# Attention and ELU feed-forward on one core: second scores joined to the next pair's tails, values into the product banks

## The chip, the cores and the metric

One core of a Trainium2 chip (trn2). The time is that of one execution on the device, in microseconds, as the median of several; lower is better. The engines are TensorE (PE; PEld is its weight load), VectorE (DVE), ScalarE (ACT), GpSimd (POOL) and SyncE (SP, which here only issues DMAs). TensorE writes to PSUM, eight banks of 512 fp32 columns on 128 partitions.

## What is computed

Threshold attention over 8 sequences of 8 heads, 576 rows of 64, and behind it a feed-forward network with an ELU, 512 to 2048 to 512, over the 4608 rows:

```python
def _attn_ref(q, k, v, tau):
    scale = 1.0 / np.sqrt(q.shape[-1])
    scores = scale * np.matmul(q, k.transpose(0, 1, 3, 2))
    thresh = np.max(scores, axis=-1, keepdims=True) - tau
    scores = np.where(scores >= thresh, scores, -1000000000.0)
    scores = scores - np.max(scores, axis=-1, keepdims=True)
    attn = np.exp(scores)
    attn = attn / (np.sum(attn, axis=-1, keepdims=True) + 1e-09)
    return np.matmul(attn, v).astype(np.float32)

def _moe_ref(x, w_in, w_out):
    h = x @ w_in
    g = np.where(h > 0.0, h, alpha * (np.exp(np.minimum(h, 0.0)) - 1.0))
    return (g @ w_out).astype(np.float32)
```

All data are fp32. Between the two, heads become columns: row (b, s) of x holds the 8 heads of that row.

## The kernel before

**Pairs.** Two heads of one sequence are a pair; there are 32, `pr` 0 to 31, four to a sequence. A pair's 576 query rows are four blocks of 128 (`i` = 0 to 3) and a tail of 64 for each head, which together make block `NC` = 4. Head h lies on partitions 64h to 64h + 63 of `qT` and `kT`.

**One block of scores** goes like this: TensorE writes 128 x 576 scores per head into PSUM (`wide_scores` L785, for the two blocks of a half, `half` 0 being blocks 0 and 1; `tails_and_values` L829 for the tails, L852). VectorE takes the negated row maximum (`wide_max` L807, at L809), POOL the threshold (`wide_bounds`, L818), ScalarE the exponential (`wide_exp`, L822) into one of two buffers (`turned_by`: `w_one` and `e`), VectorE masks and sums (`wide_mask`, L826), sums and inverts (L554, L560); POOL normalizes (L503); VectorE turns it by 32 x 32 (`turn_squares` L644, at L649 and L662), SP writes it to DRAM in pieces (`there`) and a later `fetch` (L689) reads it back transposed. Two pairs after its scores, `tails_and_values` multiplies it with v: the 64 tail rows first (L857, weights `vd`), then the four blocks (`values_main`, L865), part 1 ahead of part 0. `values_out` (L870) has ScalarE copy the result into `xt`, the input of the feed-forward network, and for part 1 into `xs`, which a DMA takes to `xtail`.

**TensorE's shapes.** Matmuls run on parts of the array. Scores, tails and the value products of the tail rows (L857) are 64x64 (four at once); the blocks' values and the FFN products of the loop (`by_columns`, L772) are 128x64 (two column halves at once). In the early stage FFN products are 128x128 (L924, L952, L992).

**PSUM.** One tile of five banks, `wide` (`sc` in the profile), takes scores, tails and values: a half's scores columns 64 to 2368; the tails banks 3 and 4, the values banks 1 and 2 before the first half's scores overwrite them. Three more banks, f0, f1 and f2 (`f`), go in turn to the FFN products (`ends`, a rotating list). `on_banks` (L744) keeps, for each bank, what touched it last on each engine, and makes an instruction wait for the other engines' accesses of its own banks alone; the tracking of the whole tile is turned off for them.

**Two stages.** The first 250 us or so (`early_tasks`, L1096: sequence 0, pairs 4 to 8, conversion of the weights, the first feed-forward rows) run jobs in an order written out by hand (`EARLY`). Jobs name what they need; `banked` hands a job's last instruction on each engine to those that need it. There a half is two jobs, `wsc.pr.half.0` and `.1`, and all jobs of the next step wait for `users`, the masks and value copies of the step before. Between the two parts of a half stands `seen` (L805), a copy of one column by ScalarE.

From pair `START` = 9 on a loop (L1798) issues work by a planned clock: `on_pe` puts a TensorE step at the planned time and moves the clock by its planned length, and everything else is put down with a due time (`at`), to be issued in the order of these times; `MOVED` and `FIRST` shift single due times. The engines wait for each other by semaphores alone, so the plan only sets the order in each engine's queue. One turn of the loop: the tails of pair pr with the values of pair pr - 2 (`tail_step` L1725); the first half of pair pr (`wide_step` L1741); 14 FFN quarters (`ffn_quarters` L1692); the second half; 14 quarters. A quarter is four matmuls of 256 columns: a seventh of a first product (`first_product` L1466, x times w_in by a scheme of seven products) or half of one of the second round's fourteen (`second_round` L1596). `sums_x` (L1086) makes the five sums of x that a group of first products needs, once a sequence.

Inputs of the next pair are turned (`prep_q`, `prep_k`) and loaded at times set from the two halves. Behind the loop the last sequence and the tails' rows have a stage of their own, in which the five banks of `wide` join the rotation.

Of the kernel before, what the change touches and what calls it, by code (L numbers as in the profile page):

```python
# [20 lines left out]
    "9:3.0": 0.61, "9:fetch0": -3.6, "9:turn4": 2.44, "e:139.1": 0.46, "e:140.2": -0.49, "e:176.2": 1.07,  # L21
    "e:203p0": 1.03, "e:30.2": 0.35, "e:73p0": 1.88, "e:75p0": 1.3, "e:77.2": -1.81, "e:78.1": -3.94, "e:9b":
# [154 lines left out]
def kernel(  # L177
# [552 lines left out]
    def followed(ins, engine, needed):  # L730
# [10 lines left out]
        serials[ins.name] = engine, len(serials), dict(have)  # L741
        return kept_

    def on_banks(made, ap):  # L744

        ins, needed, starts = made.ins, [], [ap.offset % (5 * 512)]
        for step, n in ap.ap[1:-1]:
# [20 lines left out]
    def by_columns(o, left, right, note=None, **how):  # L768
        n = o.shape[0]
        for y in range(0, n, D):  # L770
            oy = o[y : y + D] if n > D else o
            made = nc.tensor.matmul(oy, left[:, y : y + D] if n > D else left, right, skip_group_check=True, **how)  # L772
            if note:
                note(made, oy)
# [1393 lines left out]
```

## Time and profile before

| what | us |
|---|---|
| median of 3 runs | 1258.58 (1257.97 to 1258.75) |
| the profiled execution, its own time | 1258.3 |
| its span (first to last instruction) | 1256.5 |
| PE busy | 1240.8 |
| DVE busy | 1067.2 |
| POOL busy | 790.5 |
| ACT busy | 584.4 |
| granted TensorE clock, mean | 1.00 |

Busy times are unions of an engine's instructions. TensorE's ends are modelled and overlap with the next start, so its pace is read from start to start. In the view of instructions in order of time, a row is a run of like instructions: start, length, engine, line, operation, out<-in, active rows*columns of the array, operand, count, and in brackets the idle time before with what ended it. An fp32 matmul of a part of the array leaves two records.

### The profile page before, as it was taken

Reading aid. Unit: us, or ns where it says so; the run is one execution under the profiler, and the core shown is the slowest. Engines: PE = TensorE matmul, PEld = TensorE weight load, DVE = VectorE, ACT = ScalarE, POOL = GpSimd, SP = SyncE. Lnnn points to the kernel's source line nnn. Section 1 sums busy time; section 2 is a strip of 40 time slices with the busy share of each in tenths; the row PEclk is TensorE's granted clock in tenths of the full one; section 3 lists DMA queues with packets and bytes.
Section 4 is the critical chain, followed back from the end, with each engine's and each line's share of the span. In section 5 each row is a group of like instructions: output and inputs, shape, how many; then the busy total and the mean of one; then the engine's idle time right before and its main releaser. Section 6 shows DMA issues by size and latency. Waiting matters only on the chain.

```text
span 1256.5 us, 32264 instructions
## 1 busy us (share of the span) xinstructions
PE 1240.8 (99%) x11999; PEld 825.9 (66%) x11999; DVE 1067.2 (85%) x2322; ACT 584.4 (47%) x1276; POOL 790.5 (63%) x1147
## 2 busy tenths in 40 slices
PE   8999999999999999999999999999999999999998
PEld 5776575466666666666666666666666666678887
DVE  7998989898889979898889888988989885777876
ACT  7987755453444435252625353444535260434130
POOL 5775545586576747674766657674767473675564
PEclk9999999999999999999999999999999999999999
DMA  8568899898979898998989898989899876444433
GB/s 224 152 182 248 217 253 256 239 303 217 257 208 268 231 242 229 262 245 240 238 226 266 230 257 202 265 232 240 227 257 248 238 214 224 163 140 152 137 113 115
DMA packets 332940, 278.31 MB, mean 221 GB/s; under 512 B 201328, under 2 KB 288368, under 8 KB 332784
## 3 DMA queue, kind: packets, MB, share of 16 engines
q1 hardware_dynamic: 331264, 275.57, 78.6%
q8 instruction: 94, 1.54, 0.5%
q10 hardware_dynamic: 1520, 0.69, 0.2%
q14 instruction: 62, 0.51, 0.1%
HBM read 178.85 MB, written 97.32 MB: 220 GB/s over the span
## 4 chain that ended last, share of the span: by engine, by line
PE 81%; DVE 2%; DMA 1%; POOL 1%; ACT 0%; issue 0%; SPq 0%; DVEq 0%; ACTq 0%; POOLq 0%
PE f L772 59%; PE sc L865 9%; PE sc L802 8%; PE f L992 2%; PE sc L857 1%; DMA there<-x 1%; PE sc L852 1%; PE f L924 1%; DVE mx L809 1%; DVE e L826 0%; DVE x L649 0%; DVE g L1536 0%; DVE g L1508 0%; SPq L668 0%; SPq L683 0%
## 5 line engine op out<-in xcount | busy, mean ns | idle before, releaser
L809 DVE TENSOR_REDUCE mx<-sc 128x1 f32<-128x576 f32 x252 | 180.0, 745 | 35.0 <-PE sc L802 30.3
L818 POOL TENSOR_SCALAR th<-mx,ntau 128x2 f32<-128x2 f32 (+1 forms) x140 | 45.9, 328 | 185.4 <-DVE mx L809 184.3
L822 ACT ACTIVATE w_one<-sc,mx 128x576 f32<-128x576 f32 x140 | 100.8, 740 | 131.9 <-DVE mx L809 110.3
L826 DVE SCALAR_TENSOR_TENSOR w_one<-sc,th,w_one 128x576 f32<-128x576 f32 x140 | 109.9, 812 | 20.2 <-ACT w_one L822 19.0
L802 PE MATMUL sc<-kT,qT 64*64 64x320 f32 (+5 forms) x1792 | 124.5, 410 | 2.1 <-DVE su L554 0.5
L772 PE MATMUL f<-xt,sw 128*64 128x256 f32 x1024 | 123.3, 382 | 0.7 <-ACT xt L432 0.5
L822 ACT ACTIVATE e<-sc,mx 128x576 f32<-128x576 f32 x112 | 82.8, 742 | 88.1 <-DVE mx L809 86.5
L772 PE MATMUL f<-x,w_in_sb 128*64 128x256 f32 x1024 | 123.1, 380 | 0.3 <-ACT g L1547 0.3
L772 PE MATMUL f<-xt,w_in_sb 128*64 128x256 f32 x1024 | 121.8, 379 | 0.5 <-DVE xt L1092 0.5
L503 POOL TENSOR_SCALAR w_one<-w_one,rs 128x576 f32<-128x576 f32 x115 | 89.3, 787 | 38.7 <-DVE rs L560 38.7
L649 DVE STREAM_TRANSPOSE x<-w_one 128x512 f32<-128x512 f32 (+1 forms) x140 | 99.9, 743 | 15.6 <-POOL w_one L503 9.6
L802 PEld LDWEIGHTS sc<-kT,qT 64*64 64x64 f32 x1792 | 80.9, 132 | 48.9 <-issue 18.5
L772 PE MATMUL f<-w_out_sb,s 128*64 128x256 f32 (+1 forms) x896 | 105.6, 377 | 0.0
L772 PE MATMUL f<-w_out_sb,g 128*64 128x256 f32 (+1 forms) x864 | 101.7, 376 | 0.0
L772 PEld LDWEIGHTS f<-x,w_in_sb 128*64 128x64 f32 x1024 | 74.4, 137 | 37.9 <-ACT g L1547 4.8
L772 PEld LDWEIGHTS f<-xt,w_in_sb 128*64 128x64 f32 x1024 | 75.4, 137 | 35.9 <-ACT e L822 0.9
L772 PEld LDWEIGHTS f<-xt,sw 128*64 128x64 f32 x1024 | 71.9, 137 | 41.1 <-issue 5.5
L826 DVE SCALAR_TENSOR_TENSOR e<-sc,th,e 128x576 f32<-128x576 f32 x112 | 87.6, 807 | 8.0 <-ACT e L822 7.7
L772 PE MATMUL f<-t,s 128*64 128x256 f32 (+1 forms) x800 | 93.5, 375 | 0.0
L772 PEld LDWEIGHTS f<-w_out_sb,s 128*64 128x64 f32 x896 | 63.7, 137 | 31.5 <-issue 3.2
L772 PEld LDWEIGHTS f<-w_out_sb,g 128*64 128x64 f32 x864 | 61.2, 137 | 31.7 <-issue 3.7
L503 POOL TENSOR_SCALAR e<-e,rs 128x576 f32<-128x576 f32 x92 | 67.8, 741 | 20.3 <-DVE rs L560 17.8
(324 smaller groups left out, 2807.9 us busy)
## 6 DMA issues: line engine op xcount, KB each, us to landing
there<-x SPq DMA_DIRECT2D x452, 144.0 KB, 3.7
wTb<-there SPq DMA_DIRECT2D x58, 576.0 KB, 6.2
wTa<-there SPq DMA_DIRECT2D x55, 576.0 KB, 4.9
sw<-win_sums SPq DMA_DIRECT2D x62, 384.0 KB, 4.0
t<-wout_sums SPq DMA_DIRECT2D x45, 512.0 KB, 5.2
there<-x SPq DMA_DIRECT2D x112, 80.0 KB, 2.0
wTb<-there SPq DMA_DIRECT2D x56, 160.0 KB, 3.8
wst<-in_moe_w_in_dram SPq DMA_DIRECT2D x16, 512.0 KB, 5.2
```

Of the source, the lines that this page charges most:

```text
L503: nc.gpsimd.tensor_scalar(wv, wv, st["rs"][:, h : h + 1], 1.0, ALU.mult, ALU.mult)
L649: nc.vector.transpose(x[:, :, c0 : c0 + nc_], src.rearrange("p (c g n) -> p g c n", c=nc_, n=T))
L772: made = nc.tensor.matmul(oy, left[:, y : y + D] if n > D else left, right, skip_group_check=True, **how)
L802: on_banks(nc.tensor.matmul(oy, qT[r, i * P + y * D : i * P + (y + 1) * D], kT[r, k0 : k0 + n], start=True, stop=True, skip_group_check=Tr ...
L809: on_banks(nc.vector.tensor_reduce(st["mx"][:, h : h + 1], st["sc", h], axis=AX.XY if i == NC else AX.X, op=ALU.max, negate=True), st["sc" ...
L818: nc.gpsimd.tensor_scalar(st["th"][:, cs], st["mx"][:, cs], -1.0, ntau, ALU.mult, ALU.add)
L822: on_banks(nc.scalar.activation(st["e", h], st["sc", h], AF.Exp, bias=st["mx"][:, h : h + 1]), st["sc", h])
L826: on_banks(nc.vector.scalar_tensor_tensor(st["e", h], st["sc", h], st["th"][:, h : h + 1], st["e", h], ALU.is_ge, ALU.mult, accum_out=st[" ...
L852: on_banks(nc.tensor.matmul(o, qT[r, MAIN:], kT[r, TAIL + x * HALF : TAIL + (x + 1) * HALF], start=True, stop=True, skip_group_check=True), o)
L857: on_banks(nc.tensor.matmul(o, vd[r, r], parts[x][r, g0:g1, NC], start=True, stop=False, skip_group_check=True), o)
L865: on_banks(nc.tensor.matmul(o, vm[:, h, c], parts[part][:, g0:g1, h * (NC + 1) + c], start=False, stop=(c == NC - 1), skip_group_check=Tru ...
L992: nc.tensor.matmul(cur[c, i][:, :DM], hidden(c, ft % NU, 1)[:, 0, ft // NU, i], w_out_sb[:, ft], start=(ft == 0), stop=(ft == NFT - 1))
```

## The change

- `wide` gets a sixth bank, which is f0; f1 and f2 stay tiles of their own.
- In the loop a turn becomes: the second half of pair pr - 1; the tails of pair pr with the values of pair pr - 2; 14 quarters; the first half of pair pr; 14 quarters. The second half is taken in another order (`seen_too`: block 3 first, buffers exchanged) and has a second `seen` copy.
- From START on tails and values go to places of their own (`tails_apart`): tail scores to columns 2368 to 2944 (the end of bank 4 and bank 5), cut at the bank's end into 192 and 384 columns; values to f1 and f2. The list of banks is set so that f2 comes first behind the values.
- In the early stage values go to banks 4 and 0 and tails to banks 2 and 3; the first part of a first half doesn't wait for the second value copy; `seen` is no longer handed on as a thing to wait for.
- `other_banks` and `beside` turn off tracking between products in the wide tile and scores or values in its other banks; accesses of the tails in bank 5 keep it.
- The sums of x are made in two halves, the first a pair earlier (for the first group by POOL in the early stage, jobs `xe`).
- Due times of maxima, exponentials, masks, sums, turns and fetches are planned anew, and `MOVED` and `FIRST` are other tables. Before the weight sums at the end the loop issues work until the last turns are out.

```diff
-    granted, banks_at_start = [None], {x: psum["f"].tile([P, 512], FP32, name=x) for x in ("f0", "f1", "f2")}
+    granted, banks_at_start = [None], {x: psum["f"].tile([P, 512], FP32, name=x) for x in ("f1", "f2")}
...
-    wide = [psum["w"].tile([P, 5 * 512], FP32, name="sc")]
-    banks_at_start["t"] = wide[0][:, 4 * 512 :]
+    wide = [psum["w"].tile([P, 6 * 512], FP32, name="sc")]
+    banks_at_start["f0"] = wide[0][:, 5 * 512 :]
+    banks_at_start["t"] = wide[0][:, 4 * 512 : 5 * 512]
...
-        if doing[0]:
+        if doing[0] and kept:
             banked.setdefault(doing[0], {})[engine] = ins
...
+        if (max(starts) + ap.ap[-1][1] - 1) // 512 < 5:
+            if apart:
+                other_banks(ins, "scores", "products")
+            else:
+                other_banks(ins, "values", "products", (nc.scalar, nc.vector))
+                other_banks(ins, "values", "outs")
...
-            st = open_step(pr, i, turned_by[1 - s])
+            st = open_step(pr, i, turned_by[s if seen_too else 1 - s])
...
         order = (((0, 0, 0, 448), (1, 1, 0, 320), (1, 1, 320, 256), (0, 0, 448, 128)),
+                 ((1, 0, 256, 320), (0, 1, 0, 384), (1, 0, 0, 256), (0, 1, 384, 192)) if seen_too else
                  ((1, 0, 0, 256), (0, 1, 0, 384), (1, 0, 256, 320), (0, 1, 384, 192)))
...
-            if (h, s, c) == (1, 1, 0):
-                on_banks(nc.scalar.copy(seen, o[:, :1]), o[:, :1])
+            if (h, s, c) == (1, 1, 0) or seen_too and (h, s, c) == (1, 0, 256):
+                on_banks(nc.scalar.copy(seen, o[:, :1]), o[:, :1], kept=False)
...
-        pv, sc = (wide[0].rearrange("p (x n) -> p x n", n=512)[:, b : b + 2] for b in (1, 3))
+        by_bank = wide[0].rearrange("p (x n) -> p x n", n=512)
+        pv, sc = [by_bank[:, 4], by_bank[:, 0]], by_bank[:, 2:4]
+        if pr is None or pr >= START:
+            return tails_apart(pr, before)
...
+    def tails_apart(pr, before):
+
+        places = [banks_at_start[x] for x in (("f2", "f1") if pr == START else ("f1", "f2"))] if before != NP - 1 else (wide[0][:, :512], wide[0][:, 512:1024])
+        sc = wide[0][:, 2 * T + 4 * S : 2 * T + 5 * S]
...
+        cut = 5 * 512 - 2 * T - 4 * S
+        for x, c, n in ((1, cut, S - cut), (0, 0, cut)):
+            for h in range(2):
+                r = slice(h * D, (h + 1) * D)
+                if before is not None:
+                    g0, g1 = span(h, x)
+                    o = places[x][r, g0 * T : g1 * T]
+                    watch(nc.tensor.matmul(o, vd[r, r], parts[x][r, g0:g1, NC], start=True, stop=False, skip_group_check=True), o)
+                if pr is not None:
+                    o = sc[D - h * D : P - h * D, c : c + n]
+                    on_banks(nc.tensor.matmul(o, qT[r, MAIN:], kT[r, TAIL + c : TAIL + c + n], start=True, stop=True,
+                                              skip_group_check=True), o)
...
+        for x, m in enumerate(X_ORDER):
+            job(("xe", m), "pool|dve", lambda e, m=m: sum_x(m, engine_of[e]), ("outv", START - 3, 0), ("outv", START - 3, 1), "late",
+                ("xe", X_ORDER[x - 1]) if x else None)
...
-                        ("wsc", pr, half, 0) if y else ("tail", pr) if not half else ("wsc", pr, 0, 1), *ready_of[pr], *users,
+                        ("wsc", pr, half, 0) if y else ("tail", pr) if not half else ("wsc", pr, 0, 1), *ready_of[pr],
+                        *[x for x in users if y or x[0] != "outv" or x[2]],
...
+            for x in ("f1", "f0", "f2") if pr == START else ("f2", "f0", "f1"):
+                ends.remove(banks_at_start[x])
+                ends.append(banks_at_start[x])
+
+        PLANS = ({(0, 0): (0.0, 1.6, 3.0), (0, 1): (0.75, 3.0, 4.3), (1, 1): (1.5, 4.7, 6.5), (1, 0): (2.25, 5.6, 6.9)},
+                 {(0, 0): (3.4, 7.7, 8.6), (0, 1): (5.1, 6.0, 7.5), (1, 1): (-0.8, 0.2, 1.2), (1, 0): (0.1, 1.0, 2.7)})
...
-                for x, i in enumerate((NC, 0, 1, 2, 3)):
-                    at(t + 6.0 + 3.8 * x, lambda pr=pr, i=i: fetch(pr - 1, i), f"fetch{i}")
+                for i, when in ((NC, 9.0), (0, 12.5), (1, 16.0), (2, 20.0), (3, 24.0)):
+                    at(t + when, lambda pr=pr, i=i: fetch(pr - 1, i), f"fetch{i}")
...
+            if START < pr <= NP:
+                wide_step(pr - 1, 1)
             tail_step(pr)
...
-            for half in range(2):
-                if pr < NP:
-                    wide_step(pr, half)
...
+            next_q(pr)
+            ffn_quarters(HALF_QUARTERS)
+            if pr < NP:
+                e = clock[0] + 2.15
+                wide_step(pr, 0)
+                next_k(pr)
+                extras(e + 0.3, e + 1.2, e + 4.2, e + 10.4, e + 12.0)
                 ffn_quarters(HALF_QUARTERS)
```

More of the change, by code (lines that the diff above doesn't have):

```diff
@@ L771, in by_columns, with watch, other_banks, beside @@
             oy = o[y : y + D] if n > D else o
-            made = nc.tensor.matmul(oy, left[:, y : y + D] if n > D else left, right, skip_group_check=True, **how)
-            if note:
-                note(made, oy)
-    def watch(made, ap):
+            (note or beside)(nc.tensor.matmul(oy, left[:, y : y + D] if n > D else left, right, skip_group_check=True, **how), oy)
+    def watch(made, ap, apart=True):
         if ap.tensor.name == wide[0].tensor.name:
-            on_banks(made, ap)
+            on_banks(made, ap, apart)
+    def other_banks(ins, mine, theirs, engines=(nc.tensor, nc.scalar, nc.vector)):
+        for e in engines:
+            if e.engine != ins.engine:
+                tc.declare_no_dep(ins, group=f"{theirs}{e.engine}", reason="other banks")
+        tc.add_to_no_dep_group(f"{mine}{ins.engine}", ins)
+    def beside(made, ap):
+        if ap.tensor.name == wide[0].tensor.name:
+            other_banks(made.ins, "products", "scores")
+            if made.ins.engine != nc.tensor.engine:
+                other_banks(made.ins, "products", "values", (nc.scalar, nc.vector))
+        return made
     def open_step(pr, i, w):
@@ L783, in open_step, with wide_scores @@
         return st
-    def wide_scores(pr, half, parts=(0, 1)):
+    def wide_scores(pr, half, parts=(0, 1), seen_too=False):
         qT, kT, _ = pairs[pr]
@@ L1499, in copy @@
                 loc[name] = kept(name)
-                nc.scalar.copy(loc[name], place(x))
+                beside(nc.scalar.copy(loc[name], place(x)), place(x))
             def pool(name, x, other, op):
@@ L1507, in add @@
             def add(o, x, name):
[L1508 removed]
+                beside(nc.vector.tensor_tensor(o, place(x), loc[name], ALU.add), place(x))
             def exp(c):
```

198 lines of the change are left out of this document (126 added, 72 removed), and 68 rows, old and new, of tables (FIRST, MOVED).

## The prediction

> **What bounds the kernel now.** I read the page first, then the time by stretch, then TensorE's rows in order of time, then its waits.
>
> The page's head, and the stretch view (columns: length, then busy time and instructions of PE, its weight loads, DVE, ACT, POOL; clock; DMA share; GB/s):
>
> ```profile
> span 1256.5 us, 32264 instructions
> PE 1240.8 (99%) x11999; PEld 825.9 (66%) x11999; DVE 1067.2 (85%) x2322; ACT 584.4 (47%) x1276; POOL 790.5 (63%) x1147
> ```
>
> ```profile
> 100.00:255.00 155.00, 151.77 (x950) 89.45 (x952) 138.31 (x288) 94.54 (x190) 84.72 (x116) 1.00 0.88 243
> 255.00:284.00 29.00, 28.00 (x274) 17.50 (x266) 26.84 (x59) 17.00 (x38) 23.14 (x33) 1.00 0.97 295
> 284.00:1040.00 756.00, 755.89 (x7476) 480.60 (x7476) 658.16 (x1448) 330.94 (x724) 491.00 (x741) 1.00 0.88 240
> ```
>
> TensorE has 0.1 us free in the 756 us of the pair loop, at full granted clock, and VectorE 98 us. So nothing there is gained by removing a wait: only work or pace of TensorE counts. Before 284 us there are a few waits. One pair in order of time (start, length, idle before):
>
> ```profile
> 403.33 1.90 PE L772 MATMUL f<-x,w_in_sb 128*64 128x256 f32 x16
> 405.16 2.17 PE L802 MATMUL sc<-kT,qT 64*64 64x448 f32 x32
> 407.26 1.95 PE L772 MATMUL f<-xt,sw 128*64 128x256 f32 x16
> 409.04 1.03 PE L772 MATMUL f<-x,sw 128*64 128x256 f32 x8
> 409.90 1.90 PE L772 MATMUL f<-xt,w_in_sb 128*64 128x256 f32 x16
> 411.63 2.00 PE L772 MATMUL f<-x,w_in_sb 128*64 128x256 f32 x16
> 417.77 1.90 PE L772 MATMUL f<-x,w_in_sb 128*64 128x256 f32 x16
> 419.60 0.45 PE L852 MATMUL sc<-kT,qT 64*64 64x288 f32 x1
> 420.73 2.37 PE L865 MATMUL sc<-wTb,vm 128*64 128x320 f32 x16
> 422.94 1.90 PE L865 MATMUL sc<-wTa,vm 128*64 128x256 f32 x16
> 424.76 2.17 PE L802 MATMUL sc<-kT,qT 64*64 64x448 f32 x32
> ```
>
> The reader is to look at starts, since modelled ends overlap. A group of 16 FFN records lasts 1.73 us (409.90 to 411.63). If 64x64 work follows, it lasts 1.83 (403.33 to 405.16, 417.77 to 419.60); the first one behind it lasts 1.78 (407.26 to 409.04). Changing between 128x64 and 64x64 shapes thus costs time that no wait shows.
>
> The early waits, then an early score step beside the loop's 2.17, and one wait of pair 9's first products:
>
> ```profile
> PE sc L852 <- ACT xs L432: 1.0, 1, 1.0
> PE sc L802 <- ACT xt L432: 0.5, 1, 0.5
> ```
>
> ```profile
> who waited for it (us, times):
>   PEld sc L802: 3.3, 10
> ```
>
> ```profile
> 200.97 2.46 PE L802 MATMUL sc<-kT,qT 64*64 64x448 f32 x32 [0.47 <-ACT xt L432]
> 210.54 2.46 PE L802 MATMUL sc<-kT,qT 64*64 64x448 f32 x32
> ```
>
> ```profile
> 259.83 1.08 PE L772 MATMUL f<-xt,w_in_sb 128*64 128x256 f32 x8 [0.52 <-DVE xt L1092]
> ```
>
> The middle fence is the view of the one-column copy "seen" (L805): ten times, all early, the array's weight load waited for it.
>
> **The change, part by part.** *Price of a 64x64 stretch.* 16 FFN records are 2 column halves at once, so 8 x 256 = 2048 column steps in 1.73 us, 0.845 ns a step. A half's scores are 1152 columns per quadrant in two passes, 2304 steps or 1.95 us; start to start it takes 2.10, so 0.15 too much, and with 0.10 ahead and 0.05 behind 0.30. The tails (576 columns, two passes, 0.97 us) take 1.13, again 0.16 too much. Check: a pair has 28 x 1024 + 4608 + 1152 + 2 x 2304 = 39,040 steps, 33.0 us, and takes 33.9 (tails start at 419.60, 453.44, 487.38, 521.22): 0.9 over for three stretches, again 0.30 each. Bounds 0.28 to 0.31.
>
> *Second scores put behind the products, in front of the next tails.* Before, a pair has three 64x64 stretches: tails, first half, second half. After, the second half's scores and the next pair's tails (with the 64-row value products beside them) form one, and the values run on into FFN products of their own shape. Matmuls and columns are equal in number. That happens for the second halves of pairs 9 to 31, 23 times: 23 x 0.30 = **6.9 us less** (6.4 to 7.1).
>
> *Where the tails and values go.* Tail scores move to the end of bank 4 and into bank 5, which is now f0; the values go to f1 and f2. Hence the next products wait for the evacuation. Count from the end of the second half's scores, h: tails until h+1.0, values 4.03 (2.21 and 1.82 by the rows above) until h+5.0, then a quarter each 0.86. f2 is needed at h+5.0: its values end at h+3.2, the copies take 0.37 and 0.42 (ACT), so 1.0 spare. f0 is needed at h+5.9 in a first product, h+6.7 in a second round. Its user is the tail's mask. In the changed program's order the longest DVE list from the second half's first maximum to that mask is three maxima (0.74 each), a turn in two instructions (1.44), two ELUs (about 0.67), the turn of q (0.77) and the mask (0.82), 6.6 us, and a second round follows. The plan begins it 0.8 before h; in the trace of before a half's first maximum begins 1.9 to 2.25 us after the scores begin, about at their end. So the mask ends between h+5.8 and h+6.7: 0.9 to 0 spare. In the other order of pairs it is three maxima and the mask, h+3.1 at most, 2.8 spare. Half the pairs may so wait some 0.1 us: I take **1.0 us more** over the loop, bounds 0 and 5 (0.2 a pair); the old loop met like deadlines (tail mask before the first half's scores, 4 us behind the tails) with 0.1 us of idle.
>
> *What else moves.* The turns of blocks 2 and 3, their DRAM writes and their fetches come later by what the second half is later against the pair's values: fetches are planned at 9, 12.5, 16, 20, 24 instead of 6 to 21.2 us, and the values start 3.3 us into the next pair rather than 1.1, so the last transfer keeps about its 12 us; it takes some 4 to 6 us (the page's landing times). On SP's queue they stand behind the writes of the same blocks. The qm, km and v loads keep their distance to their users. 23 more seen copies of 0.16 us stand on ACT (47% busy) ahead of the copies that empty products; a value copy or exponential behind them is 1 us later, within the spare above. Sums of x split in halves: 65 DVE instructions of 0.42 for 35 of 0.68, 3.5 us on an engine with 98 us free. Nothing for these; if their cover fails it shows as waits on f0 to f2, in the bounds above.
>
> *Early stage, same order on TensorE.* The seen copy is no longer a dependence: ten steps of 2.46 come to 2.17, 2.9 us (the copy's view says 3.3 with hidden parts). The first half no longer waits for the second value copy at pairs 6 and 7, 0.47 each plus 0.06: 1.1. Tail scores leave bank 4, so the wait of 1.0 at 116.9 us goes, but DVE is busy until 117.9 and the next scores wait for its mask: 0.2. Pair 9's two runs of 14 products take 13.07 and 13.16 against 12.24: 1.75, of which the sums of x, now half done on POOL earlier, are about half. Together 5.9; DVE is 89% busy in that stretch and takes over where TensorE stops waiting, so I take **60%, 3.5 us less** (bounds 1.0 and 5.9).
>
> *Sum:* 1258.3 (the profiled execution, 1256.5 of span and 1.8 around it, which stays) - 6.9 + 1.0 - 3.5 = 1248.9. The median of the runs shown is 0.3 above that execution, so **1249.2**.
>
> **Rivals.**
>
> A. *New bank waits.* The evacuations of f0, f1, f2 come 0.2 to 0.4 us late in most pairs. For: the spare of 0 to 1.0 above, VectorE at 87%. Against: the same kind of deadline is met now. 23 x 0.3 = 6.9 gives the merger back: 1255 (1252 to 1258).
>
> B. *Slower: the joint visit is taken in turn.* Before, the two row halves of a tail visit always write different banks (x = a^h); after, both heads' tails go to one bank and both heads' values to another, on opposite partitions. If the array cannot do this at once, the visit's 0.97 us doubles: 23 x 0.97 = 22.3, so 1271. It decides from 10/23 = 0.43 us a pair on. Against: any two parts of a visit still differ in bank or in partitions. No visit of the trace has two row halves on one bank, so nothing here shows it. [...]
>
> C. *Only the early waits go.* The 0.30 belongs to each end of a shape's stretch whatever is beside it, or returns as a loss between scores and tails: 1258.6 - 3.5 = 1255. For: the price is read from neighbours, never with it gone. Against: three independent readings agree.
>
> **How the numbers follow.** Forecast 0.64 (its own range 1245.5 to 1252), A 0.18, C 0.09, B 0.09. The range of 8 in 10 reaches down to 1244 (all early waits, 0.31 a stretch, some of the end's) and up to 1257, through A and C; B is left out. A measurement here tells about 0.2% (2.5 us) from no change. Faster: forecast, C and most of A, 0.85; same 0.06; slower 0.09.
>
> **What would show it.** In the changed profile: scores followed at once by tails, about 3.2 us start to start for both, and values that run into FFN groups of 1.73; a pair every 33.6 us instead of 33.9; early score steps of 2.17; the seen view without weight loads waiting. Wrong if a pair's tail visit alone grows near 1.9 us (B), if TensorE's waits list ACT xt or DVE masks ahead of FFN products in every pair (A), or if the pair's period stays at 33.9 without waits (C).

## The result and the profile after

The changed kernel takes **1271.68 us** (median of 9 runs, 1260.06 to 1274.95), the kernel before 1258.58 (9 runs beside it, 1257.94 to 1260.95): a ratio of **1.0088**, 95% interval 1.0060 to 1.0116. The forecast was 1249.2, so it is wrong in size and in sign. The runs of the changed kernel spread over 15 us, those of before over 3. The profiled execution took 1266.71 us (span 1264.9), and the readings below are made against that one. The median lies 5.0 us above it, and what those 5.0 us are no view shows. One execution of all, the profiled one of e8 below, was disturbed and took 7334 us; it stands in no ratio.

The head of its page, and the view by stretch over the three stretches of the prediction (length, then busy time and instructions of PE, its weight loads, DVE, ACT, POOL; clock; DMA share; GB/s):

```profile
span 1264.9 us, 32319 instructions
PE 1236.5 (98%) x11999; PEld 828.6 (66%) x11999; DVE 1060.2 (84%) x2352; ACT 583.7 (46%) x1299; POOL 789.9 (62%) x1152
```

```profile
100.00:255.00 155.00, 150.24 (x949) 90.17 (x949) 138.03 (x290) 95.12 (x191) 88.69 (x121) 1.00 0.91 246
255.00:284.00 29.00, 28.53 (x292) 18.84 (x290) 18.95 (x41) 16.36 (x39) 22.02 (x30) 1.00 0.93 268
284.00:1040.00 756.00, 746.73 (x7418) 478.25 (x7414) 651.42 (x1471) 327.98 (x743) 484.57 (x737) 1.00 0.87 237
```

The same matmuls keep TensorE busy 4.3 us less than before (1236.5 for 1240.8), as the change was meant to do. But in the loop it had 0.1 us free, and now has 756.00 - 746.73 = 9.3. Something makes it wait. First a pair in which nothing does (instructions in order of time):

```profile
417.92 2.17 PE L835 MATMUL sc<-kT,qT 64*64 64x448 f32 x32
419.91 0.43 PE L931 MATMUL f<-wTb,vd 64*64 64x320 f32 x1
419.91 0.49 PE L934 MATMUL sc<-kT,qT 64*64 64x384 f32 x2
...
420.99 2.37 PE L942 MATMUL f<-wTb,vm 128*64 128x320 f32 x16
423.19 1.90 PE L942 MATMUL f<-wTa,vm 128*64 128x256 f32 x16
424.92 1.90 PE L793 MATMUL f<-w_out_sb,g 128*64 128x256 f32 x16
```

Start to start, the second half's scores take 1.99 us (2.10 before), the tails' visit 1.08 (1.13), the values 3.93 (4.03). The next tails begin at 453.43, 33.52 behind 419.91, where before the mean was 33.93. The joined stretch does what was predicted, and somewhat more.

Now the waits, who waited for what: us in total, times, longest. First after, then before; the turns' line is L664 after and L649 before, the fetches' line is L708 and L693:

```profile
DVE x L664 <- DMA there<-x: 30.0, 15, 4.3
...
SPq L708 <- DMA there<-x: 65.6, 37, 4.4
```

```profile
DVE x L649 <- DMA there<-x: 4.4, 3, 2.1
...
SPq L693 <- DMA there<-x: 2.9, 4, 1.3
```

A turn writes its block into one of two buffers (`squares`, called rooms below), from which four DMAs carry it to DRAM. "DVE waits for there<-x" says that VectorE is about to turn a block and both rooms are still being emptied. "SP waits for there<-x" says that a fetch stands on SP's queue until the turned block that it is to read has landed; what is queued behind it waits too. Such a place after, VectorE's instructions first, then SP's:

```profile
393.89 0.71 DVE L664 STREAM_TRANSPOSE x<-w_one 128x512 f32<-128x512 f32 x1
...
397.12 1.44 DVE L664 STREAM_TRANSPOSE x<-e 128x640 f32<-128x640 f32 x2
402.81 1.44 DVE L664 STREAM_TRANSPOSE x<-w_one 128x640 f32<-128x640 f32 x2 [4.25 <-DMA there<-x]
```

```profile
393.36 0.42 SPq L368 DMA_DIRECT2D vm<-in_v_dram  x1
...
396.79 1.91 SPq L683 DMA_DIRECT2D there<-x  x4
398.74 0.44 SPq L708 DMA_DIRECT2D wTa<-there  x1
399.23 3.53 SPq L354 DMA_DIRECT2D qm<-in_k_dram  x4
402.80 1.38 SPq L708 DMA_DIRECT2D wTa<-there  x1
404.28 0.38 SPq L1136 DMA_DIRECT2D sw<-win_sums  x1
404.75 4.91 SPq L698 DMA_DIRECT2D there<-x  x8
412.30 0.81 SPq L708 DMA_DIRECT2D wTb<-there  x2
```

The tail is turned at 393.89, block 3 at 397.12, and block 2 would follow at 398.56 (397.12 + 1.44). The tail's writes leave SP only at 396.79, 1.8 us behind the end of its turn, since loads are ahead of them; the last lands at 402.69, and block 2 gets the room at 402.81. VectorE, in order, did nothing for 4.25 us. Its writes and block 3's leave together (x8): block 3's too had stood behind loads and a fetch, 6.2 us from the end of its turn (398.56) to 404.75. The fetches of both (412.30) come at the very moment at which the last write has landed (412.16). They land at 417.73, 2.2 us ahead of the products that read them (419.91). In a pair of before, the tail's turn and the two behind it:

```profile
428.35 0.70 DVE L649 STREAM_TRANSPOSE x<-w_one 128x512 f32<-128x512 f32 x1
...
436.46 1.43 DVE L649 STREAM_TRANSPOSE x<-e 128x640 f32<-128x640 f32 x2
437.82 1.44 DVE L649 STREAM_TRANSPOSE x<-w_one 128x640 f32<-128x640 f32 x2
```

There 8 us lie between the tail's turn and the next, and the tail's writes have landed at 432.93.

What TensorE then waits for is VectorE's work that came late, ahead of the next products (`sc` in a row of L793 is f0, `f` is f1 or f2):

```profile
PE sc L793 <- DVE su L569: 3.2, 6, 0.6
...
PE sc L793 <- DVE g L1606: 2.3, 5, 0.6
PE f L793 <- DVE ot L1741: 1.8, 3, 1.2
```

So the waits stand where the prediction looked for them, at f0 to f2. But VectorE isn't late there by the plan: of TensorE's 18 waits between 284 and 1040 us, 15 end within 10 us after VectorE got a room that it had stood for (402.81 is followed by 404.61, 406.14 and 412.59), and the 11 of 22 pairs that keep 33.5 to 33.6 us have no wait for a room of more than 0.64 us.

At the end of the loop there is one wait of another kind, in the visit of pair 31's values:

```profile
1066.66 0.83 PE L931 MATMUL sc<-wTb,vd 64*64 64x320 f32 x4 [2.43 <-issue]
1067.22 1.12 PE L931 MATMUL sc<-wTa,vd 64*64 64x256 f32 x4
1068.28 3.52 PE L942 MATMUL sc<-wTb,vm 128*64 128x320 f32 x16
```

After 2.43 us without work, the first value part takes 3.35 us (its starts 1068.28 and 1071.63) instead of 2.21.

### The profile page after: what moved, and what is told of

It reads as the page before. It is cut to its first block, busy times and chain, and to the rows that moved or that the text cites. A ratio compares the mean times of both kernels' runs of the same rounds, so it can differ in the third digit from the quotient of the medians.

```text
span 1264.9 us, 32319 instructions
## 1 busy us (share of the span) xinstructions
PE 1236.5 (98%) x11999; PEld 828.6 (66%) x11999; DVE 1060.2 (84%) x2352; ACT 583.7 (46%) x1299; POOL 789.9 (62%) x1152
## 4 chain that ended last, share of the span: by engine, by line
PE 76%; DMA 7%; DVE 7%; SPq 4%; issue 3%; ACT 2%; POOL 1%; DVEq 0%; ACTq 0%; POOLq 0%
PE f L793 39%; PE sc L793 11%; PE sc L835 7%; PE f L942 7%; DMA there<-x 3%; PE f L1070 2%; PE sc L1070 2%; DMA wTb<-there 2%; PE f L931 2%; DVE mx L842 1%; PE sc L510 1%; PE f L1029 1%; DMA wTa<-there 1%; DVE x L664 1%; DVE g L1634 1%
## 5 line engine op out<-in xcount | busy, mean ns | idle before, releaser
L664 DVE STREAM_TRANSPOSE x<-w_one 128x512 f32<-128x512 f32 (+1 forms) x140 | 99.8, 743 | 38.4 <-DMA there<-x 28.7
L859 DVE SCALAR_TENSOR_TENSOR w_one<-sc,th,w_one 128x576 f32<-128x576 f32 x140 | 111.3, 811 | 18.9 <-ACT w_one L855 9.9
L835 PE MATMUL sc<-kT,qT 64*64 64x256 f32 (+5 forms) x1792 | 121.6, 409 | 4.4 <-DVE w_one L859 4.3
L835 PEld LDWEIGHTS sc<-kT,qT 64*64 64x64 f32 x1792 | 79.2, 132 | 50.4 <-issue 17.0
L793 PE MATMUL f<-w_out_sb,s 128*64 128x256 f32 (+1 forms) x896 | 105.8, 377 | 1.8 <-DVE ot L1741 1.8
L793 PE MATMUL f<-x,w_in_sb 128*64 128x256 f32 x832 | 100.9, 379 | 0.0
L859 DVE SCALAR_TENSOR_TENSOR e<-sc,th,e 128x576 f32<-128x576 f32 x112 | 88.6, 809 | 9.3 <-ACT e L855 6.1
L793 PE MATMUL f<-xt,sw 128*64 128x256 f32 x736 | 91.7, 381 | 2.0 <-DVE g L1606 1.5
L793 PE MATMUL f<-t,s 128*64 128x256 f32 (+1 forms) x800 | 93.5, 375 | 0.0
L793 PE MATMUL f<-xt,w_in_sb 128*64 128x256 f32 x736 | 90.9, 380 | 0.0
L793 PEld LDWEIGHTS f<-w_out_sb,s 128*64 128x64 f32 x896 | 63.4, 137 | 34.3 <-DVE ot L1741 3.4
L838 ACT COPY seen<-sc 128x1 f32<-128x1 f32 x79 | 12.6, 159 | 157.6 <-PE sc L835 157.6
L664 DVE STREAM_TRANSPOSE x<-e 128x640 f32<-128x640 f32 x108 | 77.5, 755 | 5.5 <-POOL e L518 2.6
L793 PEld LDWEIGHTS f<-x,w_in_sb 128*64 128x64 f32 x832 | 61.9, 137 | 27.9
L793 PEld LDWEIGHTS f<-t,s 128*64 128x64 f32 x800 | 57.2, 137 | 28.0
L793 PEld LDWEIGHTS f<-xt,sw 128*64 128x64 f32 x736 | 53.1, 137 | 29.7 <-DVE g L1606 3.3
```

The costliest lines, as they stand in the source:

```text
L664: nc.vector.transpose(x[:, :, c0 : c0 + nc_], src.rearrange("p (c g n) -> p g c n", c=nc_, n=T))
L793: (note or beside)(nc.tensor.matmul(oy, left[:, y : y + D] if n > D else left, right, skip_group_check=True, **how), oy)
L835: on_banks(nc.tensor.matmul(oy, qT[r, i * P + y * D : i * P + (y + 1) * D], kT[r, k0 : k0 + n], start=True, stop=True, skip_group_check=Tr ...
L859: on_banks(nc.vector.scalar_tensor_tensor(st["e", h], st["sc", h], st["th"][:, h : h + 1], st["e", h], ALU.is_ge, ALU.mult, accum_out=st[" ...
```

## The experiments

All ratios are to the kernel before, run beside each on the same chip, with 95% intervals.

### More time for the third turn, fewer loads in the way, an earlier end

My first theory was that block 2's turn only stands in a bad place of the plan. **e1_turn2_later** moved it by 3.9 us (pairs of odd number) and 1.9 (even), and its fetch by more, 9.0 and 7.1:

```diff
-    "fturn2": 5.56, ... "sfetch2": 1.94, "sfetch3": 0.48, ... "sturn2": 7.56,
+    "fturn2": 9.5, "ffetch2": 9.0, ... "sfetch2": 9.0, "sfetch3": -0.5, ... "sturn2": 9.5,
```

> The turn of block 2 is put about 4 us (odd pairs) and 2 us (even pairs) later in VectorE's order, its fetch with it; nothing else. Theory 1 (two rooms for three turns: the third turn, block 2's, stands in VectorE's queue until the tail block's write to DRAM has landed, and everything behind it is late): VectorE's waits on landings of there<-x fall from 30.0 us (15 times) below 10, the tails of pairs 10 to 32 come over 743 to 746 us instead of 752.4, and the time falls by 6 to 9 us. Theory 2 (the evacuations of f0, f1, f2 miss their deadlines by the plan itself, whatever the turns do): the waits on landings fall, but TensorE's waits on VectorE ahead of FFN products stay, and the time is within 2 us of the changed kernel's.

**e2_v_later** took the v loads out of the tail's way:

```diff
-                at(t + 9.0, lambda pr=pr: load(pr, ("v",)))
+                at(t + 20.0, lambda pr=pr: load(pr, ("v",)))
```

> The four loads of v are put on SP's queue 11 us later, behind the writes of the tail's and block 3's turns. Theory 1 with SP's queue as part of the price: the tail block's four writes start some 2 us after its turn less (they now start 1.8 us after it, behind four loads of v), so the waits of 2 to 4 us on landings shrink by about 2 each, 15 to 20 us of VectorE in all, and the time falls by 3 to 6 us. If only the landing itself counts (about 4 us from the write's start), nothing changes beyond 2 us. Theory 2: nothing changes.

**e3_last_half_early** issued pair 31's second half within turn 31, ten quarters behind its first half (`if pr == NP - 1: ffn_quarters(10); wide_step(pr, 1); ffn_quarters(4)`), and **e4_all_three** had the three edits together.

> Only pair 31's second half goes back to the place before (in the middle of the last 14 products), all else as changed. If the end is lost because the last pair's turns and fetches are a quarter of a turn of the loop late and nothing stands behind them: the wait of 2.4 us ahead of the last tail products and the granted clock of 0.65 behind it both go, tails of pair 32 to 33 take 29.3 to 29.8 instead of 31.8, the rest behind 196.7 instead of 198.3, so 3 to 4 us less. If the half clock has another cause than the idle time, only 2 us less.

> The three edits together. Theory 1: 10 to 14 us less than the changed kernel, 1257 to 1262 or below the kernel before if the waits go whole (its clean pairs take 33.52 instead of 33.93, 9 us over 22 pairs). Theory 2: 3 to 5 us less, from the end alone.

Measured: e1 1324.04 (ratio 1.0537, 1.0494 to 1.0581), e2 1284.79 (1.0202, 1.0164 to 1.0240), e3 1271.76 (1.0116, 1.0072 to 1.0161), e4 1344.54 (1.0677, 1.0647 to 1.0708). None beat the changed kernel, and three of the four were slower than it by 13 us and more. In e1 VectorE's wait for rooms all but went, and this came instead:

```profile
DVE x L665 <- DMA there<-x: 3.7, 3, 1.9
...
PE f L932 <- DMA wTb<-there: 21.4, 12, 3.0
PE f L932 <- issue: 10.1, 3, 5.9
```

The values now wait for the fetch. In e2 likewise the rooms' waits fell to 14.0 us, and `PE f L931 <- DMA wTb<-there: 15.3, 7, 3.5` came in. e3 left the fetches' due times, so the values of pair 31 waited 3.7 us for them all the same. The theory fell in this form: by its plan a turn can't be put later for nothing, since the values behind it then wait for the fetch. e1 doesn't tell whether the later turn or the much later fetch made them wait.

### Taking the two suspects away, one at a time and together

Three kernels leave something out to show what it costs. **e5_old_fetch** lets each fetch read what the pair before wrote; **e6_tail_unsent** doesn't write the tail's turned block; **e9_both** has the two together.

```diff
+        if pr >= START:
+            back, olds[i] = olds.get(i, back), back
```

```diff
+                send = turn_squares(pr, i)
+                if i == NC and pr > START:
+                    turns[pr, i] = first_tail[0]
+                else:
+                    send()
```

> From the first pair of the loop on, each fetch reads the DRAM tile that the pair before wrote, so it never waits for the writes of its own turn to land; bytes, turns and transfers are the same in number. The output's values are made with the weights of the pair before. Theory H (the later second half leaves too little time for the way turn, write, fetch, values; the single queue of SP then stands in fetches that wait for landings, and writes behind them leave late): SP's waits for its own landings (65.6 us in the changed kernel) go to below 15, VectorE's waits for the rooms of its turns (30.0 us) to below 8, and pairs come every 33.5 to 33.7 us: 1247 to 1256. Rival R (the three turns in a row need a third room whatever SP waits for): VectorE's waits stay at 20 us or more and the time at 1263 or above.

> From the second pair of the loop on, the tail block's turned squares are not written to DRAM (the fetch reads the first pair's tile), so their room is free at once; four writes of 80 KB a pair are left out, and the output's tails are made with the first pair's weights. Rival R (rooms): VectorE's waits for rooms fall from 30.0 to below 8 us, and most of the 15 us of stalls in pairs 10 to 32 goes: 1256 to 1262. Theory H: the rooms come free sooner, but the fetches of blocks 2 and 3 still wait for their landings (SP over 35 us of 65.6), and half or more of the stalls stay: 1262 to 1270.

> Both of the earlier cuts at once: fetches read what the pair before wrote (no wait for their own landing), and the tail's turned squares are not written (four writes a pair left out, their room free at once). If landings and rooms are the whole of what the loop lost, VectorE waits for no room (below 3 us), SP for no landing (below 10 us), pairs come every 33.5 us, and the time is what the prediction had, 1247 to 1251. If something else stalls the loop (masks, banks, the tail of the pipeline at pair 32), it stays at 1252 or above.

Measured: e5 1256.37 (0.9984, 0.9972 to 0.9995), e6 1252.01 (0.9955, 0.9938 to 0.9971), e9 **1248.04** (0.9912, 0.9899 to 0.9924). Their turns' and fetches' waits, in this order:

```profile
DVE x L664 <- DMA there<-x: 18.2, 10, 3.6
```

```profile
SPq L709 <- DMA there<-x: 61.0, 39, 3.9
...
DVE x L664 <- DMA there<-x: 2.4, 3, 1.7
```

```profile
284.00:1000.00 716.00, 716.00 (x7168) 465.40 (x7166) 632.67 (x1430) 315.91 (x711) 468.19 (x709) 1.00 0.88 234
```

The last is e9's view by stretch: TensorE has nothing free in 716 us of the loop, and every pair from 10 to 32 takes 33.52 or 33.53. Tail starts, pair by pair, give the account:

| stretch (tails' starts), us | before | after | e5 | e6 | e9 |
|---|---|---|---|---|---|
| tail of pair 9 begins at | 248.38 | 247.77 | 246.56 | 245.66 | 246.12 |
| pair 9 to 10 | 35.59 | 34.67 | 34.87 | 34.91 | 34.67 |
| 22 pairs, 10 to 32 | 746.55 | 752.44 | 744.93 | 738.74 | 737.59 |
| 32 to 33 | 29.32 | 31.78 | 31.07 | 31.67 | 31.45 |
| 33 to the end | 196.66 | 198.26 | 196.67 | 198.46 | 196.54 |
| span | 1256.5 | 1264.9 | 1254.1 | 1249.4 | 1246.4 |

What the loop lost is 752.44 - 737.59 = 14.85 us, and the two cuts together give all of it back. In e5 SP's waits for landings at the fetches are 5.4 us. Alone, free rooms for the tail give 13.7, though SP still stands 61.0 us in its fetches; fetches that needn't wait give 7.5, while rooms still cost 18.2 us of VectorE. So neither of the two theories as I had put them was right by itself. The reading that fits both runs: the missing room is what stops VectorE, and SP's standing costs by holding back the writes that empty the rooms. (e6 and e9 also have 4 issues and 320 KB a pair less, so a part of their gain may be theirs. A kernel with a third room, the direct test, was not run.)

### The early edits alone

**e7_early_only** is the kernel before with the early edits (tails in banks 2 and 3, values in banks 4 and 0, `kept=False`, the second value copy left out of `users`).

> The kernel before with the early edits alone: the one-column copy is no dependence, tail scores in banks 2 and 3 and values in banks 4 and 0, and the first half does not wait for the second value copy. The prediction's step of 3.5 us (bounds 1.0 and 5.9) gives 1252.7 to 1257.6; if VectorE takes over where TensorE stops waiting, 1257 to 1259. In either case the loop's pairs keep 33.93 us.

Measured 1258.81 against 1258.94 (1.0003, 0.9993 to 1.0012): no difference. The tail of pair 9 begins at 245.23, 3.15 us earlier than before; but 22 pairs take 749.97 instead of 746.55. My expectation of 33.93 a pair missed that in the kernel before the loop uses the same tail and value places: of the 22 first score steps eight now last 2.34 to 2.46 us instead of 2.10, start to start, where before one does. That is some 1.8 us of the 3.4 given back; the rest I didn't trace. The changed kernel has places of its own in the loop and doesn't pay this.

### The other half joined

If the last turns lack time, the **first** half can be joined to its own pair's tails, and the second stay where it was. Then the same number of stretches goes, and the last turns keep their distance to the values. **e8_first_half_joined**:

```diff
-            if START < pr <= NP:
-                wide_step(pr - 1, 1)
+            if START < pr < NP:
+                wide_step(pr, 0, 1)
...
+            if pr == START:
+                wide_step(pr, 0)
             ffn_quarters(HALF_QUARTERS)
             if pr < NP:
                 e = clock[0] + 2.15
-                wide_step(pr, 0)
+                wide_step(pr, 1)
```

The edit has two more parts: pair 31's fetches go back to the due times of before (the last one 21.2 us into the turn instead of 24), and one copy of k is due earlier (`skcopy`).

> The half that is put ahead of a pair's tails is that pair's own first half, instead of the second half of the pair before; the second half stays 14 products into its pair, as before the change. The joined stretches are equal in number (23 or 22), the last turns of a pair have some 47 us again until their values. Theory H: tails every 33.5 to 33.6 us, VectorE's waits for rooms below 10 us, no late fetch at pair 32: 1245 to 1252, faster than both. Rival R (three turns in a row at the joined stretch fill two rooms, whichever half it is): VectorE's waits stay above 20 us and the time is 1258 or more. A third possibility: the first half's evacuation collides with the pair's own tail masks, TensorE then waits for masks ahead of products at f0 to f2, 1256 to 1265.

> The same kernel as in the run before it, whose profiled execution was disturbed (7332 us); wanted is a clean profile. Median 1256 to 1260. Theory H+R (landings and rooms both): no wait of SP for landings of its own (below 15 us, since the last turns have 33 us until their values), but VectorE's waits for rooms at 10 us or more, since the joined half's two turns and the tail's still come one behind another. If instead VectorE's waits are below 5 us, the loss is elsewhere (masks ahead of products, or early).

Measured: e8 1258.35 (0.9994, 0.9983 to 1.0005), and the same kernel again as e10 1261.12 (1.0016, 1.0000 to 1.0032). In e10's profile SP's fetches wait 5.1 us for landings instead of 65.6, and 32 to 33 takes 29.32 again, but `DVE x L664 <- DMA there<-x: 17.8, 9, 3.0` stays: 22 pairs take 743.73. (One of these pairs, 31 to 32, has only one half in it and takes 32.24, so the least is 21 x 33.53 + 32.24 = 736.4.) The first pair of the loop takes 40.05. The last turns of a pair have some 31 us until their values (turned by 491.18, used at 522.35), not the 47 that I expected. So the time to the values was cured, the rooms were not: three turns still follow one another wherever a half is joined to tails.

**e16_first_half_tail_unsent** bounds the rest, as e6 did:

> First half joined, and from the second pair of the loop on the tail's turned squares are not written (four writes a pair left out, the output's tails made with the first pair's weights), so that its room is free at once. This bounds what the rooms cost here: 1249 to 1254 if they are what is left; 1257 or more if the loss is at the loop's beginning (the first pair took 40.05 us) or in masks ahead of products.

Measured 1250.31 (0.9931, 0.9918 to 0.9944), 22 pairs 736.92: in the loop, the tail's writes and the room that they hold are all that was left. (As in e6, 4 issues and 320 KB a pair are gone with them.)

### Writes from another queue

**e11_first_half_tail_on_act** (on e8) and **e12_tail_on_act** (on the changed kernel) issue the tail's four writes from ScalarE's queue:

```diff
+                if i == NC:
+                    at(now[0] + 1.5, lambda: go(nc.scalar))
```

> First half joined, and the tail's four writes issued from ScalarE's queue 1.5 us behind its turn by the plan, instead of on SP's, where they stand behind loads. Same bytes. If the rooms are what is left of the loss, the tail's room comes free 1 to 2 us sooner in each pair: 1250 to 1256. If ScalarE's exponentials are held up by its wait for the turn, 1257 to 1262.

> The changed kernel with the tail's four writes issued from ScalarE's queue (as in the run before). The room comes free 1 to 2 us sooner, and SP has four issues less in the crowded stretch: VectorE's waits for rooms fall from 30 us to 10 to 20, and the time to 1257 to 1266. Nothing changes (1268 to 1275) if SP's order is without weight.

Measured: e11 1385.56 (1.1022, 1.0999 to 1.1044), e12 1393.03 (1.1061, 1.1043 to 1.1078), both far outside what was expected. SP's waits in e12:

```profile
SPq L370 <- DMA there<-x: 78.1, 12, 9.7
SPq L712 <- DMA there<-x: 72.4, 14, 8.4
SPq L708 <- DMA there<-x: 57.6, 36, 4.3
```

L370 loads a v tail and L712 fetches a tail. VectorE's waits for rooms fell to 14.4 us, as expected, but the time did not follow. In one place L712's second DMA stood from 490.57 to 498.98 on SP, until the first of the writes that ScalarE had issued from 496.53 on, those of the next tail, had landed (498.96): a write that it doesn't read. The trace also has, for each DMA, the semaphore that its landing raises and those that it waits for, and these tell the cause. All DMAs of e12, from both queues, take turns on eight semaphores (100 to 107); beside the waits for its data, a DMA waits for the one that had its semaphore before. (In the changed kernel's trace 1361 of SP's 1368 DMAs have the next of the eight, and 1179 wait for their own.) ScalarE's write has semaphore 104, and so has the DMA of L712, which waits for 104. In 22 places of e12 SP stood over 1 us, 147.1 us in all, until a write of ScalarE's that had the same semaphore had landed (e11: 23 places, 154.8 us); in the changed kernel there is no such place. So a wait came in with the edit that the writes on SP's own queue don't cause, and SP's order itself was not tested.

### Towards a kernel that keeps the gain

With the first half joined, nothing is near its landing, so the moves that failed in e1 and e2 could be tried again: the third turn, here block 0's, later (e13: `fturn2` 8.0, `sturn2` 9.5), v loads at 20 (e14), both (e15).

> First half joined, and the third turn of the joined stretch planned 2.4 us (odd order) and 1.9 us later, so that VectorE does other work instead of waiting for the room. The fetches stay; here they are 10 us and more behind the landings. If the rooms are the loss that is left in the loop (743.7 us for pairs 10 to 32 against 737.4 without any wait), VectorE's waits for rooms fall from 17.8 to below 8 us and the time to 1251 to 1256. If the shift only hands the delay on to the next user of the same weights, 1258 or more.

> First half joined, and the v loads planned at 20 us into the pair instead of 9, so that the tail's writes leave SP at once. In the changed kernel the same move made fetches late (1284.8); here no fetch is near its landing, so it can't: VectorE's waits for rooms fall from 17.8 to below 10 us, 1252 to 1257. If the move itself costs, whatever the fetches' slack, 1265 or more.

> First half joined with both moves of the two runs before. Rooms theory: waits for rooms below 4 us, 1249 to 1254, faster than both kernels. Otherwise no better than the better of the two.

Measured: e13 1263.11 (1.0035, 1.0023 to 1.0047), e14 1260.64 (1.0017, 1.0003 to 1.0032), e15 1263.44 (1.0037, 1.0025 to 1.0049). All three missed. In e13 the rooms' waits are gone (2.0 us), and pairs of even number take 33.52 to 33.58, yet the odd ones take 34.57 or more (but for the last, which has one half). VectorE in such a pair:

```profile
407.63 0.41 DVE L1606 TENSOR_TENSOR g<-sc,s 128x256 f32<-128x256 f32 x1
407.97 1.42 DVE L664 STREAM_TRANSPOSE x<-w_one 128x640 f32<-128x640 f32 x2
409.32 2.04 DVE L842 TENSOR_REDUCE mx<-sc 128x1 f32<-128x576 f32 x3
```

The turn now stands ahead of the next half's maxima and moves them by its 1.4 us. TensorE then waits at f0 for the tail's sums (`PE sc L793 <- DVE su L569: 5.8, 10, 0.7`), and such a pair takes 1.05 us more; that the one makes the other is my reading of the order. In e14 loads that were moved came late instead (`PE f L931 <- DMA qm<-in_q_dram: 3.8, 3, 2.1`). So I moved the turn in pairs of even number alone (`sturn2` 9.5, `fturn2` left at 5.56), and in a second kernel spread the first pair's score steps too (6, 11 and 11 quarters):

> First half joined, the third turn planned later in pairs of even number alone. Even pairs 33.53 us throughout, odd ones as with the first half joined (stalls of 1 to 1.6 us in every second of them, some 5 us in all): profiled span 1253 to 1256, median 1255 to 1260. If odd pairs stall more than before, the rooms' waits have only been handed to the next pair.

> As the run before it, and in the loop's first pair 6 quarters of products stand between the values and the first half's scores, then 11 and 11 instead of 14 and 14. If the 3.4 us of stalls in that pair come from ScalarE's copies standing behind the exponentials of score steps too close to one another, the first pair falls from 40.05 to 37 to 38.5 us and the time by 2 to 3 us against the run before: 1253 to 1257, faster than before by 0.2 to 0.4%. If not, no change, or slower by new stalls in pair 10.

Measured: **e17 1255.03 (0.9968, 0.9956 to 0.9980)**, e18 1255.29 (0.9971, 0.9957 to 0.9985). Both leave nothing out, and both beat the kernel before by 0.3%. That is little: e8 and e10, one and the same kernel on two chips, differ by 0.2%, and e17 and e18 ran on one chip alone. Against the changed kernel e17 is 0.9968 / 1.0088 = 0.988. How much of that is the even turn isn't settled: e10's profile and e17's have the same span (1255.7), though 22 pairs take 741.79 in e17 and 743.73 in e10, and VectorE still waits 16.3 us for rooms (17.8 in e10). e18's second edit did not do what it was meant for: the first pair takes 40.40 instead of 40.06.

## Why the prediction was wrong

The sum, term by term, against the profiled executions (before 1258.3, after 1266.71):

| term | predicted | measured | where |
|---|---|---|---|
| joined stretches | -6.9 | -9.0 | 22 pairs, e9 against before (the 23rd is in the row of pair 9) |
| waits on f0 to f2 | +1.0 | 0 | same pairs, no wait in e9 |
| early stage and pair 9 | -3.5 | -1.5 | (247.77 - 248.38) + (34.67 - 35.59) |
| turns, writes, fetches | 0 | +14.9 | 22 pairs, after against e9 |
| pair 31's fetch | 0 | +2.5 | 31.78 - 29.32 |
| last stage | 0 | +1.6 | 198.26 - 196.66 |
| sum | -9.4 | +8.5 | the executions differ by 8.4 |

**The step that failed is "What else moves".** It held that the turns, writes and fetches of blocks 2 and 3 would cost nothing, that "the last transfer keeps about its 12 us", and that what failed there would show as waits on f0 to f2, within a bound of 5. It compared due times of fetches with the start of the values, and left out two things that stand ahead of a fetch. One is the whole way since the turn: in a pair of before, blocks 2 and 3 were turned by 453.67 and used at 487.38, 33.7 us; after, turned by 404.25 and used at 419.91, 15.7. The fetches of before found their data landed long since and waited 2.9 us in all on SP; those of after wait 65.6 for the landing itself, with other blocks' writes behind them. The last fetch issued 9.7 us ahead of the values before (477.68), and 7.2 after (412.75). The other is the two rooms: the step saw "the writes of the same blocks" on SP's queue, but not that tail, block 3 and block 2 now come to be turned within 5 us, and that a room is held for the time of the queue and the landing (7.7 us for the tail, 394.99 to 402.69). What failed did show as waits on f0 to f2, but the loop lost 14.9 us by it and not 5 at most. e9 shows that with both out of the way the gain is there. That its 1248.0 lies so near the 1249.2 is in part luck: the loop gained 9.0 where 5.9 were forecast, and the end of the loop lost 2.1 that nobody had counted.

**The price of a 64x64 stretch** was right in its mechanism and too small: 8.96 / 22 = 0.41 us a pair instead of 0.30, outside my bounds of 0.28 to 0.31. The scores give 0.11, the tails 0.05, the values 0.10; of the two runs of 14 quarters in a pair of e9 one takes 12.19 and the other 12.24, before 12.24 and 12.24 to 12.34, which is some 0.1 together. I had not counted that the values too lose an end, since products of their own shape follow them. My own rows had it: the values' 4608 steps are 3.89 us at 0.845 ns, and they took 4.03.

**Where the tails and values go**: the deadline at f0 with "0.9 to 0 spare" holds, in e9, in every pair. The 1.0 was not needed.

**The early stage** gains less than the 3.5. In the 18 profiles of kernels with the changed early program, the tail of pair 9 begins at 244.79 to 247.77, median 246.35: 0.6 to 3.6 earlier than before's one profile, 2.0 in the middle; the profile after, from which the 1.5 comes, has the least of them. The 0.92 of pair 9 itself holds one joined stretch, some 0.4. Score steps take 2.17 as predicted, but new waits for masks came (`PE sc L835 <- DVE w_one L859: 4.3, 3, 1.7`).

**The end of the loop** was not costed at all. With the second half joined, pair 31's last fetch is planned 24 us into a turn that takes only 29 us, and the values wait: 31.07 to 33.37 us for 32 to 33 in e3, e5, e6 and e9, 29.32 in e10, where the first half is joined and these fetches have the due times of before. e3 has the half back in turn 31 but not the due times: its last block's writes had landed by 1057.98, yet the last fetch issued at 1063.77 and landed at 1069.85, and the values began at 1069.98. After the 2.43 us without work the granted clock was 0.59 (below), which is most of the last stage's 1.6: from the values' first instruction to the next products after's visit takes 7.33 us (1066.66 to 1073.99), e9's 5.78.

**Rivals.** A (f0 to f2 late in most pairs by 0.2 to 0.4, 1255) named the place where TensorE waits, but not the cause: half the pairs lose 0.1 us at most, the others up to 2.7 us, mostly behind a missing room, and in e9 none waits. C (only the early waits go) falls with pairs of 33.52. B (the joint visit taken in turn, 1271) lies next to the measured time, and is refuted: the visit of tails and values, both row halves in one bank, takes 1.08 us in the changed kernel and not 1.94. With the row halves in one bank, on opposite partitions of it, the trace shows no price: the visit took 1.13 us before, where they wrote different banks. A time near a rival's is no evidence for it: the profile decided, by the visit's own length.

## What to carry to other kernels

When a step is moved, follow its data to the last reader, and write down for each buffer on the way how long it is held (queue, transfer, landing) and how many holders now meet; a due time that still lies ahead of its reader says nothing of that. SP's queue served in order here, so what stood behind its 65.6 us of waits for landings left late (block 3's writes, behind loads and a fetch, 6.2 us after the end of their turn). And to see whether a gain exists at all, leave the suspects out together, in a kernel made for that alone: e9 showed in one run that the mechanism was sound, and so that a different arrangement was worth looking for.

## What the runs showed of the hardware that was not expected

**TensorE's granted clock fell behind an idle time of 2.43 us and not behind one of 2.10.** Stretches around pair 31's values, after and e9 (the column behind the busy times is the granted clock):

```profile
1064.00:1066.60 2.60, 0.24 (x4) 0.00 (x0) 1.34 (x3) 0.00 (x0) 0.83 (x1) 1.00 1.01 389
1066.60:1070.00 3.40, 3.34 (x16) 1.52 (x18) 1.85 (x5) 0.00 (x0) 0.00 (x0) 0.59 1.03 422
```

```profile
1047.00:1049.80 2.80, 0.73 (x8) 0.21 (x5) 1.84 (x4) 0.00 (x0) 0.83 (x1) 1.00 0.99 398
1049.80:1053.00 3.20, 3.17 (x24) 1.91 (x26) 1.85 (x5) 0.00 (x0) 0.00 (x0) 1.00 1.02 416
```

2.43 us without work were followed by 0.59 of the clock, 2.10 by all of it. At the same visit in two other profiles 1.7 us were followed by 1.00 (e5, 1057.40 to 1060.50) and 2.3 us by 0.51 (e6, 1051.00 to 1054.00). From what length on the clock falls, these four places don't show.

**Writes issued from a second queue made SP wait for them** (e12, 78.1 and 72.4 us), in instructions that don't read what was written: DMAs of both queues take turns on the same eight semaphores in this program (100 to 107), and SP stood until a write of ScalarE's with the same semaphore as its own DMA had landed (22 places, 147.1 us).
